# Growth and state products of the first units on VectorE, more filler matmuls, and a new table of positions, in an attention and MLP kernel on one Trainium2 core

## The chip, the core and the metric

The kernel runs on one core of a Trainium2 chip. Its engines are TensorE (PE, with its weight loads as PEld), VectorE (DVE), ScalarE (ACT), GpSimd (POOL) and SyncE (SP); SyncE issues every DMA that matters here. The metric is the device time of one launch in microseconds, median of several runs: 646.78 for the kernel before (three runs, 645.94 to 647.84).

## The reference

A gated linear recurrence with a complex decay runs over 768 steps for 4 batches of 8 heads with head size 48. Its output is the input of an MLP of width 384 to 2048 to 384.

```python
mag = np.sqrt(a_re * a_re + a_im * a_im)
scale = np.minimum(mag, 0.999) / (mag + 1e-06)
...
for t in range(S):
    ...
    S_re, S_im = (new_re + kv, new_im)
    y[:, :, t] = np.einsum('bhd,bhde->bhe', q[:, :, t], S_re)
...
h = x @ w_in
sp = np.where(h > 20.0, h, np.log1p(np.exp(np.minimum(h, 20.0))))
g = h * np.tanh(sp)
return (g @ w_out).astype(np.float32)
```

## The kernel before

The sequence is cut into 12 units of 256 steps (three to a batch), each of two chunks of 128. A unit passes through three blocks of work.

- **Elementwise** (`ew_steps`). From `a_re` and `a_im` it makes the running magnitude (scans at line 333, exponentials on ScalarE, tile X) and the running angle (scans at line 347, reduction to one turn at lines 353 to 358, sine and cosine in `X1` and `R` on ScalarE). `grow` (line 378) multiplies q and k, in tile QK, by the two exponentials in X; this is the growth product. Two tiny copies on GpSimd (lines 380 and 381) follow. `rot` (line 400) then makes four products with sine and cosine, and `relay` (line 391) sends the results by DMA into tile T, with heads and real and imaginary parts on the partitions: per unit six DMAs `T<-X` and six `T<-QK`.
- **Attention** (`attn_steps`). Per chunk: transposes of k (`pkn`, line 465), the products of q and k (`pa`, line 473, masked into `am` on VectorE at line 476), the output in `ypsum` (line 489), and the state update `upd`: matmuls `pd` (line 505), a copy or addition on VectorE (lines 509 and 511), then the product S times the decay at the chunk's end (line 513); this is the S product. `fin` copies the unit's output with four DMAs `xf<-y` (line 524) and splits it into a high part `xH` (ScalarE) and a low part `xL` (VectorE, line 159).
- **MLP** (`moe_steps`). Eight pairs of steps per unit: 18 matmuls into `ph` (line 551), a chain over ScalarE and VectorE (lines 556 to 561, results `g`, `gh`, `gl`), 12 matmuls into `po` (line 581).

The weights arrive as 64-bit floats and are converted in 24 pieces, w_in in `raw`, w_out in `wraw` (two buffers): one ScalarE copy, two VectorE operations (lines 191 and 195), one integer addition on GpSimd (line 200), one cast on ScalarE or VectorE (line 158), one subtraction on VectorE (line 159). Units 0 and 1 run their MLP in halves, since the second halves of the weights come later.

Which engine makes a product is fixed in the code: the growth product is on VectorE for unit 0 alone and on GpSimd for all others, the S product likewise. `spin` issues matmuls on constant data into a scratch bank, whose result nobody reads; they keep TensorE busy. There are 18 before the first attention, after the first angle reduction (`turned[0]`), and 12 more behind unit 0's last attention output (`copied[0]`).

The order of all work comes from a plan: each step is put at a number (the tables EW, AT, LD, WP give first and last positions for a unit's elementwise steps, attention steps, loads and weight conversions), and ES, TS, WS, MB and the per-step table SHIFT move the step's priority. A scheduler then writes one instruction list per engine, SyncE's DMA list among them; each engine works through its list in order and waits at an entry whose inputs are not there.

Of the kernel before, what the change touches and what calls it, by code (L numbers as in the profile page):

```python
# [22 lines left out]
ALU = mybir.AluOpType  # L23
# [18 lines left out]
GACT = 0  # L42
GATE = -1
GRP = 2
RG, QG, GN = 5, 1, 0
SQ0, SORD, CGA, CGN, CGD, ACTG = 1, 0, 9, 3, 0, 0
YDVE = []
RQ = [(), ()]
LG, WG = 12, 12
W1 = 0  # L50
ADDV = 12
NACT, MAGP = 2, 0
ROTU = 2
ROTP = [2]
TREE = 1
WRB, WI = 2, 512
FIN0 = -3.09
FS = 0.0
TRUNC = 0
AFTERX = 0  # L60
# [2 lines left out]
MULP = 0  # L63
LONG = 2
WIDE = 1
WREP, WREP2, WK = 18, 12, -8.6
FAST = [0, 1]
EW = [(-16.09, -10.95), (-12.73, -8.83), (-13.6, -11.78), (-17.88, -11.79), (-16.56, -10.6)]
AT = [(-7.62, -4.55), (-3.79, -0.81), (-8.05, -2.82), (-8.41, -3.06), (-10.49, -2.73)]
WP = [(-7.98, -3.4), (-2.51, 2.77), (1.94, 7.2), (9.3, 9.35)]  # L70
WS = [-3.58, -1.77, 0.05, 1.02]
ES = [3.85, -0.83, -1.67, 1.33]
TS = [0.58, -1.31, 2.46, -0.05]
MB = [-1.21, -0.14]
WL1 = -1.83
SHIFT = {32: -0.19, 113: 0.04, 229: 0.63, 252: 0.1}
RB = 2
XB, X1B = 2, 2
LD = [(-17.86, -17.24, -16.49), (-18.78, -19.85, -19.81), (-17.97, -17.71, -17.6), (-21.23, -15.07, -17.56), (-24.18, -15.85, -17.38)]
WL = 512  # L80
XRUNS = ((0, 0, 0, 32), (0, 1, 32, 16), (64, 1, 64, 16), (0, 2, 80, 32))
LOW, HIGH, FADED = 0.55, 2e6, 1e-17
# [5 lines left out]
def tile_kernel(ctx, tc, q, k, v, are, aim, w_in, w_out, out):  # L88
    nc = tc.nc
# [141 lines left out]
    def ew_steps(u):  # L231
# [141 lines left out]
        def both(x, g):  # L373
            return x[:, g].rearrange("p j a t -> p (j a) t" if isinstance(g, int) else "p c j a t -> p (c j a) t")

        def grow(g):
            QK, X = both(st["QK"], g), both(st["X"], g)
            (nc.vector if g in FAST and u == 0 else nc.gpsimd).tensor_tensor(  # L378
                QK[..., :C], QK[..., :C], X[..., :C], ALU.mult)
            nc.gpsimd.tensor_copy(QK[..., C:], X[..., C - 1:C])  # L380
            nc.gpsimd.tensor_copy(X[..., C:], X[..., C - 1:C])
            q2 = flat(st["QK"][:, :, :, 0], g)[:, :, C]
            cnt = ew.tile([P, NJ * NCH], F32, tag="cnt", name="cnt", bufs=1)
            nc.vector.tensor_scalar(cnt[:, :q2.shape[1]], q2, FADED, 0.0, ALU.is_ge, ALU.add,
                                    accum_out=good[:, gi(g), 2:3])
# [58 lines left out]
    def attn_steps(u):  # L444
# [8 lines left out]
        def chunk(c):  # L453
            first = uu == 0 and c == 0
            last = uu == NU - 1 and c == NCH - 1
            cs = slice(c * C, (c + 1) * C)
            d = {}

            def kn(g):
                def f():  # L460
                    if g == 0:
                        d["kn"] = at.tile([P, H, 2 * D], F32, tag="kn", name="kn")
                    pt = bank([P, 4, 2 * D], "kn", "pkn", c)
                    for i in range(4):
                        nc.tensor.transpose(pt[:, i, :], st["T"][c][:, 4 * g + i, 1, :C], ident[:2 * D, :2 * D])
                    nc.scalar.copy(d["kn"][:, 4 * g:4 * g + 4, :], pt)
                return f

            def amat(g):
                def f():  # L470
                    pa = bank([P, 4, C], "am", "pa", c)
                    for i in range(4):
                        nc.tensor.matmul(pa[:, i, :], st["T"][c][:, 4 * g + i, 1, :C],  # L473
                                         st["T"][c][:, 4 * g + i, 0, :C], start=True, stop=True)
                    am = d["am", g] = at.tile([P, 4, C], F32, tag="am", name="am", bufs=2)
                    nc.vector.tensor_tensor(
                        am, pa, cmask.unsqueeze(1).broadcast_to([P, 4, C]), ALU.mult)
                return f

            def yv(g):  # L480
                def f():
                    py = ypsum
                    for i in (2 * g, 2 * g + 1):
                        for n, old in enumerate(((True, False), (False, True))[u < WIDE] if not first else (False,)):
                            for par in range(2):
                                h = 2 * i + par
                                lhs = d["S"][:, h, :] if old else st["V"][:, c, h * D:(h + 1) * D]
                                rhs = st["T"][c][:, h, 0, :C] if old else d["am", h // 4][:, h % 4, :]
                                nc.tensor.matmul(py[64 * par:64 * par + D, i, :], lhs, rhs,  # L489
                                                 start=n == 0, stop=first or n == 1)  # L490
                    if g == 1:
                        if c == 0:
                            st["y"] = at.tile([112, 4, TU], F32, tag="y", name="y", bufs=1)
                        ins = (nc.vector.tensor_copy if u < 1 and c in YDVE else nc.scalar.copy)(st["y"][:, :, cs], py)
                        if u == 0 and c == 1:
                            copied.append(ins)
                return f

            def upd():
                nS = at.tile([2 * D, H, D], F32, tag="S", name="S", bufs=2)  # L500
                for g in range(2):
                    pd = bank([2 * D, 4, D], "pd", "pd", c)
                    for i in range(4):
                        h = 4 * g + i
                        nc.tensor.matmul(pd[:, i, :], d["kn"][:, h, :], st["V"][:, c, h * D:(h + 1) * D],  # L505
                                         start=True, stop=True)
                    sl = slice(4 * g, 4 * g + 4)
                    if first:
                        nc.vector.tensor_copy(nS[:, sl, :], pd)
                    else:  # L510
                        nc.vector.tensor_tensor(nS[:, sl, :], pd, d["S"][:, sl, :], ALU.add)  # L511
                pe = st["T"][c][:, :, 0, C].unsqueeze(2).broadcast_to([2 * D, H, D])
                (nc.vector if u < WIDE else nc.gpsimd).tensor_tensor(nS, nS, pe, ALU.mult)  # L513
                state["S"] = nS

            def take():
                d["S"] = state.get("S")

            return ([] if last else [kn(0), kn(1)]), [amat(0), amat(1)], [take, yv(0), yv(1)], [] if last else [take, upd]
# [92 lines left out]
    for u in range(NUN):  # L612
        slot = slots.get(u, range(NPAIR * u, NPAIR * (u + 1)))
        t0 = slot[0]
        place(ew_steps(u), t0 + EW[min(u, len(EW) - 1)][0], t0 + EW[min(u, len(EW) - 1)][1], ES[min(u, 3)])
        for n, f in enumerate(units[u]["load"]):
            x = t0 + LD[min(u, len(LD) - 1)][n]
            plan.append((x, len(plan), f, x))
        asteps = attn_steps(u)
        if u == 0:  # L620
            plan.append((FIN0, len(plan), asteps.pop(), FIN0 + FS))
        place(asteps, t0 + AT[min(u, len(AT) - 1)][0], t0 + AT[min(u, len(AT) - 1)][1], TS[min(u, 3)])
        moe = moe_steps(units[u], u * TU, u, u < 2)
        for j in range(NPAIR):
            plan.append((slot[j], len(plan), moe[0][j], slot[j] + MB[0]))
            plan.append((slot[j] + LAG + 0.5, len(plan), moe[1][j], slot[j] + LAG + 0.5 + MB[1]))
    edge = len(plan)
    plan.append((-15.9, len(plan), load_win(0)))
    plan.append((WL1, len(plan), load_win(1)))
    plan.append((WK, len(plan), spin(WREP, turned)))  # L630
    if WREP2:
        plan.append((FIN0 + 0.01, len(plan), spin(WREP2, copied)))
    n = HALF // WI
    for i, f in enumerate((win, wout)):
        for half in range(2):
            place([f(n * half + m) for m in range(n)], *WP[2 * half + i], WS[2 * half + i])
    def due(x):
        key = x[1] if x[1] < edge else 1000 + x[1] - edge
        return (x[3] if len(x) > 3 else x[0]) + SHIFT.get(key, 0.0), x[1]

# [23 lines left out]
def general(tc, nc, q, k, v, are, aim, pools, moe_steps, split):  # L664
    io, ew, at, ps, dram = (pools[n] for n in ("io", "ew", "at", "ps", "dram"))
    BJ = B * NJ
    TS = 8
    xs = dram.tile([B, S, DM], F32, name="xs")
# [14 lines left out]
    kv, t1, t2, t3, t4 = w1[:, 0], w1[:, 1], w2[:, 0], w2[:, 1], w3  # L683
    n = B * TS * D
    m = BJ * TS
    big = at.tile([P, n + 5 * m], F32, tag="T", name="big", bufs=TB)
    more = at.tile([P, 3 * m + BJ * D], F32, tag="T", name="more", bufs=TB)
    vb = big[:, 0:n].rearrange("p (b t e) -> p b t e", b=B, t=TS)
    cols = [x[:, o + i * m:o + (i + 1) * m].rearrange("p (b j t) -> p b j t", b=B, j=NJ)
            for x, o, cnt in ((big, n, 5), (more, 0, 3)) for i in range(cnt)]  # L690
    cq, ck, cr, ci, cm, ca, cb, cc = cols
    qs = more[:, 3 * m:].rearrange("p (a e) -> p a e", e=D)
    ysb = at.tile([H, B, TS, D], F32, tag="T", name="ysb", bufs=TB)
    tt, ts = nc.vector.tensor_tensor, nc.vector.tensor_scalar
# [132 lines left out]
```

## Time and profile before

| | |
|---|---|
| median of 3 runs | 646.78 us |
| profiled execution, its own time | 646.22 us |
| its span, first to last instruction | 644.4 us |
| mean granted TensorE clock | 0.958 of full speed |
| busy: PE / DVE / ACT / POOL | 579.0 / 500.3 / 493.4 / 124.2 us |

Busy time is the sum over an engine's instructions; the rest of the span it is idle. The page's slices show that TensorE is busy nine tenths or more from about a third of the span on, at the full clock, and less, at changing clocks, before. A granted clock of 1.0 is 2.4 GHz, one of 0.5 is 1.2 GHz. In the rows below a bracket behind an instruction names the idle time before it and what ended that wait.

### The profile page before, as it was taken

To read this page: it belongs to the slowest core of one execution; us is meant where nothing else is said; L and a number is where in the kernel's file an instruction comes from. 1 tells how busy PE (TensorE), PEld (TensorE's weight loads), DVE (VectorE), ACT (ScalarE), POOL (GpSimd) and SP (SyncE) were. 2 spreads that over 40 slices of the span, in tenths; PEclk is the share of its full clock that TensorE was granted. 3 is DMA by queue.
4 is the path that set the end of the run, shared out by engine and by line. 5 is a ranking of instruction groups with operands and counts; after the bars stand their busy time and mean duration, and the time that the engine had idled before them with its cause. 6 is when DMAs were issued, how large, how long until landed. Compare 5 with 4: busy or idle time off the path is not lost.

```text
span 644.4 us, 11738 instructions
## 1 busy us (share of the span) xinstructions
PE 579.0 (90%) x4480; PEld 547.3 (85%) x4480; DVE 500.3 (78%) x859; ACT 493.4 (77%) x789; POOL 124.2 (19%) x99
## 2 busy tenths in 40 slices
PE   0597963987799999999999999999999999999996
PEld 0386853987789999989999999999999999999995
DVE  6979999999879868777878698688588786534451
ACT  7968876877696987978888887888789868655561
POOL 2433364325103103103003112111031030000000
PEclk9958977897899999999999999999999999999999
DMA  8877434514821530630711712703702503101000
GB/s 304 264 255 219 120 115 121 166 37 130 222 64 50 148 100 25 158 89 26 194 54 48 181 45 61 190 22 95 177 23 63 138 14 95 42 25 26 1 26 30
DMA packets 58528, 67.05 MB, mean 104 GB/s; under 512 B 4960, under 2 KB 51040, under 8 KB 58464
## 3 DMA queue, kind: packets, MB, share of 16 engines
q1 hardware_dynamic: 58464, 66.23, 36.1%
q8 instruction: 37, 0.61, 0.4%
q14 instruction: 27, 0.22, 0.1%
HBM read 36.96 MB, written 5.51 MB: 66 GB/s over the span
## 4 chain that ended last, share of the span: by engine, by line
PE 36%; DVE 27%; ACT 17%; DMA 9%; issue 6%; SPq 4%; POOL 1%; DVEq 0%; ACTq 0%; POOLq 0%
PE po L581 14%; PE ph L551 13%; ACT e L124 7%; DVE gl L159 3%; ACT L132 3%; PE ypsum L489 3%; DVE e L556 3%; PE pa L473 3%; DMA T<-QK 3%; SPq L391 3%; ACT X L124 2%; DMA R<-a_re 2%; PE pd L505 2%; DVE g L561 2%; DMA xf<-y 2%
## 5 line engine op out<-in xcount | busy, mean ns | idle before, releaser
L581 PE MATMUL po<-wo,gh 128*128 128x384 f32 x768 | 219.2, 347 | 13.8 <-DVE wo L158 10.4
L551 PE MATMUL ph<-xH,wiH 128*128 128x256 f32 x576 | 168.7, 294 | 3.7 <-DVE g L561 3.6
L551 PE MATMUL ph<-xL,wiH 128*128 128x256 f32 x576 | 165.1, 287 | 4.4 <-DVE xL L159 4.4
L551 PE MATMUL ph<-xH,wiL 128*128 128x256 f32 x576 | 165.5, 288 | 0.0
L581 PEld LDWEIGHTS po<-wo,gh 128*128 128x128 f32 x768 | 141.4, 190 | 18.4 <-DVE wo L158 10.7
L124 ACT ACTIVATE e<-e 128x512 f32<-128x512 f32 x192 | 119.6, 629 | 46.8 <-DVE e L556 44.7
L581 PE MATMUL po<-wo,gl 128*128 128x384 f32 x384 | 131.0, 341 | 0.0
L551 PEld LDWEIGHTS ph<-xH,wiH 128*128 128x128 f32 x576 | 111.5, 194 | 8.4 <-issue 4.8
L551 PEld LDWEIGHTS ph<-xL,wiH 128*128 128x128 f32 x576 | 111.5, 194 | 5.3 <-DVE xL L159 5.2
L551 PEld LDWEIGHTS ph<-xH,wiL 128*128 128x128 f32 x576 | 111.3, 193 | 0.2 <-issue 0.2
L556 DVE TENSOR_SCALAR e<-e 128x512 f32<-128x512 f32 x96 | 55.3, 577 | 40.8 <-ACT e L124 40.5
L561 DVE SCALAR_TENSOR_TENSOR g<-e,ph 128x512 f32<-128x512 f32 x96 | 65.5, 682 | 21.0 <-ACT e L124 20.1
L124 ACT ACTIVATE e<-ph 128x512 f32<-128x512 f32 x96 | 56.6, 590 | 30.8 <-PE ph L551 28.8
L159 DVE TENSOR_TENSOR gl<-g,gh 128x512 fp32r<-128x512 f32 x96 | 74.5, 776 | 1.6
L513 POOL TENSOR_TENSOR S<-S,T 96x384 f32<-96x384 f32 x18 | 26.6, 1476 | 240.0 <-DVE S L511 91.6
L581 PEld LDWEIGHTS po<-wo,gl 128*128 128x128 f32 x384 | 72.8, 190 | 0.0
L124 ACT ACTIVATE e<-e,fifth 128x512 f32<-128x512 f32 x96 | 69.1, 720 | 1.8
L158 DVE CAST gh<-g 128x512 fp32r<-128x512 f32 x96 | 42.8, 445 | 33.9 <-PE po L581 32.6
L378 POOL TENSOR_TENSOR QK<-QK,X 128x1536 f32<-128x1536 f32 (+1 forms) x12 | 40.9, 3412 | 123.8 <-ACT X L124 123.8
L132 ACT ACT_TABLE_LOAD x45 | 57.7, 1283 | 1.6 <-PEq L783 0.8
L473 PE MATMUL pa<-T 96*128 96x128 f32 x384 | 51.4, 283 | 4.5 <-DVE S L511 3.4
L473 PEld LDWEIGHTS pa<-T 96*128 96x128 f32 x384 | 48.3, 197 | 5.2 <-DVE S L511 3.5
(88 smaller groups left out, 820.1 us busy)
## 6 DMA issues: line engine op xcount, KB each, us to landing
T<-X SPq DMA_DIRECT2D x72, 129.0 KB, 2.5
T<-QK SPq DMA_DIRECT2D x72, 129.0 KB, 4.3
raw<-w_in SPq DMA_DIRECT2D x12, 512.0 KB, 8.2
wraw<-w_out SPq DMA_DIRECT2D x12, 512.0 KB, 3.6
QK<-q SPq DMA_DIRECT2D x12, 384.0 KB, 4.0
QK<-k SPq DMA_DIRECT2D x12, 384.0 KB, 4.7
V<-v SPq DMA_DIRECT2D x12, 384.0 KB, 4.9
out_dram<-o SPq DMA_DIRECT2D x24, 192.0 KB, 1.9
```

The lines of the kernel that those rows point to most:

```text
L124: ins = nc.scalar.activation(out, in_, func, **kw)
L132: ins = nc.scalar.preload_act_table_set(name)
L158: heng(h, src)
L159: leng(out=lo, in0=src, in1=h.bitcast(F32), op=ALU.subtract)
L378: (nc.vector if g in FAST and u == 0 else nc.gpsimd).tensor_tensor(QK[..., :C], QK[..., :C], X[..., :C], ALU.mult)
L391: ins = (nc.gpsimd if u == 0 and 3 * cs + j in RQ[c] else nc.sync).dma_start(rows[cs * NJ + j], src[:, c, j])
L473: nc.tensor.matmul(pa[:, i, :], st["T"][c][:, 4 * g + i, 1, :C], st["T"][c][:, 4 * g + i, 0, :C], start=True, stop=True)
L513: (nc.vector if u < WIDE else nc.gpsimd).tensor_tensor(nS, nS, pe, ALU.mult)
L551: nc.tensor.matmul(ph[:, a, :], wi[wp][:, j, kt, a * P:a * P + P], st[xp][:, kt, :], start=n == 0, stop=n == 8)
L556: nc.vector.tensor_scalar_min(e, e, math.exp(20.0))
L561: nc.vector.scalar_tensor_tensor(g, e, 2.5, ph, ALU.subtract, ALU.mult)
L581: nc.tensor.matmul(po[t], gp[:, a, tsl], wo[part][:, wp, 2 * i + a, :], start=j in starts and a == 0 and n == 0, stop=j + 1 in ends and a ...
```

## The change

Growth products of units 1 to 3 and S products of units 1 and 2 go from GpSimd to VectorE. The rounding of the angle in units 0 and 1 (line 353, ScalarE) becomes line 355 on VectorE (NACT). The fillers grow from 18 to 24 and from 12 to 18. Conversion of the first weights is ordered behind unit 0's first four rotation products (CGD), unit 1's first squares behind unit 0's sines (ACTG), and the second half of w_in is no longer held behind unit 1's q and k loads and unit 0's output copy (QG, RG). All positions are new, and SHIFT has 74 entries where it had 4.

```diff
-RG, QG, GN = 5, 1, 0
-SQ0, SORD, CGA, CGN, CGD, ACTG = 1, 0, 9, 3, 0, 0
+RG, QG, GN = 9, 0, 0
+SQ0, SORD, CGA, CGN, CGD, ACTG = 1, 0, 9, 3, 4, 1
-NACT, MAGP = 2, 0
+NACT, MAGP = 0, 0
-FIN0 = -3.09
+FIN0 = -2.9
-WREP, WREP2, WK = 18, 12, -8.6
-FAST = [0, 1]
-EW = [(-16.09, -10.95), (-12.73, -8.83), (-13.6, -11.78), (-17.88, -11.79), (-16.56, -10.6)]
-AT = [(-7.62, -4.55), (-3.79, -0.81), (-8.05, -2.82), (-8.41, -3.06), (-10.49, -2.73)]
...
+WREP, WREP2, WK = 24, 18, -9.4
+FASTU, FASTE, SPE = 4, 99, 3
+EW = [(-15.98, -11.16), (-12.71, -8.85), (-13.64, -11.75), (-17.88, -11.94), (-16.2, -10.54)]
+AT = [(-9.7, -6.15), (-4.54, -2.43), (-8.86, -3.46), (-7.13, -3.62), (-10.18, -2.73)]
...
-SHIFT = {32: -0.19, 113: 0.04, 229: 0.63, 252: 0.1}
...
-LD = [(-17.86, -17.24, -16.49), (-18.78, -19.85, -19.81), (-17.97, -17.71, -17.6), (-21.23, -15.07, -17.56), (-24.18, -15.85, -17.38)]
+LD = [(-16.55, -15.97, -14.96), (-17.84, -19.05, -19.66), (-18.09, -17.59, -17.24), (-20.15, -13.15, -18.75), (-24.2, -15.53, -17.4)]
...
-            (nc.vector if g in FAST and u == 0 else nc.gpsimd).tensor_tensor(
+            (nc.vector if u < FASTU or u >= FASTE else nc.gpsimd).tensor_tensor(
                 QK[..., :C], QK[..., :C], X[..., :C], ALU.mult)
...
-                (nc.vector if u < WIDE else nc.gpsimd).tensor_tensor(nS, nS, pe, ALU.mult)
+                (nc.vector if u < SPE else nc.gpsimd).tensor_tensor(nS, nS, pe, ALU.mult)
```

The table of numbers tells a reader nothing of the order, so three places of the instruction lists follow, before and with the change. The first is VectorE's list around unit 2's growth product, from the unit's magnitude scan on (R: magnitude and then cosine, X: exponentials, wiL and wo: weights). Before:

```order
L333 SCALAR_TENSOR_TENSOR R<-rmask,R 128x768
L355 TENSOR_SCALAR I<-X_738 128x768
L195 SCALAR_TENSOR_TENSOR wraw<-wraw,wx 128x512
L561 SCALAR_TENSOR_TENSOR g<-e,ph 128x512
L159 TENSOR_TENSOR xL<-xf,xH 128x256 x3
L356 SCALAR_TENSOR_TENSOR I<-X_738,I 128x768
L191 TENSOR_SCALAR wx<-raw_99 128x512
L158 CAST gh<-g 128x512
L195 SCALAR_TENSOR_TENSOR raw_99<-raw_99,wx 128x512
L159 TENSOR_TENSOR gl<-g,gh 128x512
L159 TENSOR_TENSOR wo_491<-wraw,wo_491 128x512
L191 TENSOR_SCALAR wx<-wraw 128x512
```
With the change:

```order
L333 SCALAR_TENSOR_TENSOR R<-rmask,R 128x768
L355 TENSOR_SCALAR I<-X_794 128x768
L561 SCALAR_TENSOR_TENSOR g<-e,ph 128x512
L159 TENSOR_TENSOR xL<-xf,xH 128x256 x2
L195 SCALAR_TENSOR_TENSOR wraw<-wraw,wx 128x512
L159 TENSOR_TENSOR wiL<-raw_99,wiH 128x512
L159 TENSOR_TENSOR xL<-xf,xH 128x256
L356 SCALAR_TENSOR_TENSOR I<-X_794,I 128x768
L158 CAST gh<-g 128x512
L378 TENSOR_TENSOR QK<-QK,X 128x12x128
L384 TENSOR_SCALAR cnt,good<-QK 128x6
L191 TENSOR_SCALAR wx<-raw_99 128x512
```
The product L378, which GpSimd made before and which is not in VectorE's list before, now stands nine rows behind the scan L333 whose exponentials it needs, in front of the check of its result (L384).

The second place is SyncE's list where unit 3's relays, unit 2's output copies `xf<-y` and the next loads meet. Before:

```order
L391 DMA T<-X 16x8x258 x2
L219 DMA wraw<-w_out 128x512
L391 DMA T<-X 16x8x258 x4
L391 DMA T<-QK 16x8x258 x6
L263 DMA V<-v 128x768
L248 DMA R<-a_re 128x768
L256 DMA QK<-q 128x6x128
L524 DMA xf<-y 128x1x256
L524 DMA xf<-y 64x1x256 x2
L524 DMA xf<-y 128x1x256
L256 DMA QK<-k 128x6x128
```
With the change:

```order
L391 DMA T<-X 16x8x258
L219 DMA wraw<-w_out 128x512
L391 DMA T<-X 16x8x258 x5
L391 DMA T<-QK 16x8x258 x2
L263 DMA V<-v 128x768
L391 DMA T<-QK 16x8x258 x3
L524 DMA xf<-y 128x1x256
L524 DMA xf<-y 64x1x256 x2
L524 DMA xf<-y 128x1x256
L391 DMA T<-QK 16x8x258
L248 DMA R<-a_re 128x768
L256 DMA QK<-q 128x6x128
```
The output copies stood behind the loads V, R and q; now they stand in front of R and q and of the last relay.

The third is the same list one unit later (relays of unit 4, loads of R two units ahead), and it repeats for five more units with the load of R at a similar place. Before:

```order
L248 DMA I<-a_im 128x768
L391 DMA T<-X 16x8x258 x6
L524 DMA xf<-y 128x1x256
L524 DMA xf<-y 64x1x256 x2
L524 DMA xf<-y 128x1x256
L263 DMA V<-v 128x768
L391 DMA T<-QK 16x8x258 x6
L248 DMA R<-a_re 128x768
```
With the change:

```order
L248 DMA I<-a_im 128x768
L391 DMA T<-X 16x8x258 x4
L248 DMA R<-a_re 128x768
L391 DMA T<-X 16x8x258 x2
L524 DMA xf<-y 128x1x256
L524 DMA xf<-y 64x1x256 x2
L524 DMA xf<-y 128x1x256
L263 DMA V<-v 128x768
L391 DMA T<-QK 16x8x258 x6
```
The load of R moved from behind the twelve relays to behind the fourth of them.

## Rows read from the trace of the kernel before

**Rows 1.** Five stretches: us, busy (count) of PE, PEld, DVE, ACT, POOL, clock, DMA share, GB/s.

```profile
20.00:50.00 30.00, 25.26 (x151) 18.24 (x150) 26.25 (x53) 24.48 (x51) 13.01 (x9) 0.73 0.74 242
50.00:110.00 60.00, 42.20 (x313) 36.49 (x311) 58.79 (x90) 46.14 (x74) 29.10 (x19) 0.87 0.50 143
110.00:160.00 50.00, 41.63 (x285) 39.54 (x286) 50.00 (x81) 38.13 (x60) 18.66 (x12) 0.84 0.36 107
160.00:182.00 22.00, 17.27 (x127) 16.06 (x126) 17.03 (x30) 15.08 (x29) 2.57 (x2) 0.92 0.75 193
182.00:600.00 418.00, 413.64 (x3353) 399.15 (x3352) 316.80 (x546) 333.77 (x519) 56.70 (x39) 1.00 0.31 82
```

**Rows 2.** Chain that ended last, 0 to 52 us: start us, us, what.

```profile
4.93 6.64 DMA raw<-w_in
18.67 0.51 ACT I L353
```

**Rows 3.** The same chain, 80 to 185 us.

```profile
159.84 5.47 DMA wraw<-w_out
173.50 4.17 DMA xf<-y
```

**Rows 4.** GpSimd (POOL) in order of time: start us, us, instruction [idle before].

```profile
93.19 3.66 POOL L378 TENSOR_TENSOR QK<-QK,X 128x1536 f32<-128x1536 f32 x1
144.46 4.15 POOL L378 TENSOR_TENSOR QK<-QK,X 128x1536 f32<-128x1536 f32 x1 [6.42 <-ACT X L124]
154.19 1.03 POOL L513 TENSOR_TENSOR S<-S,T 96x384 f32<-96x384 f32 x1
```

**Rows 5.** VectorE (DVE) in order of time, beside those GpSimd instructions.

```profile
93.43 3.69 DVE L159 TENSOR_TENSOR xL<-xf,xH 128x256 fp32r<-128x256 f32 x1
145.16 3.46 DVE L358 COPY ncar<-I 128x3 f32<-128x3 f32 x1
154.44 1.07 DVE L158 CAST gh<-g 128x512 fp32r<-128x512 f32 x1
```

**Rows 6.** VectorE instructions grouped by line and form: count, busy us, mean ns, idle before.

```profile
L378 DVE TENSOR_TENSOR QK<-QK,X 128x768 f32<-128x768 f32 x2 | 1.9, 960 | 0.8 <-ACT X L124 0.8
L328 DVE TENSOR_SCALAR X<-X 128x384 f32<-128x384 f32 x2 | 0.8, 418 | 0.0
L513 DVE TENSOR_TENSOR S<-S,T 96x384 f32<-96x384 f32 x2 | 1.1, 568 | 0.0
L159 DVE TENSOR_TENSOR xL<-xf,xH 128x256 fp32r<-128x256 f32 x27 | 11.1, 420 | 3.5 <-ACT xH L158 3.3
L358 DVE COPY ncar<-I 128x3 f32<-128x3 f32 x5 | 0.8, 160 | 0.0
L158 DVE CAST gh<-g 128x512 fp32r<-128x512 f32 x96 | 42.8, 445 | 33.9 <-PE po L581 32.6
```

**Rows 7.** VectorE in order of time, 30 to 50 us, with its idle time.

```profile
38.68 0.35 DVE L509 COPY S<-pd 96x192 f32<-96x192 f32 x1 [1.60 <-PE pd L505]
43.84 0.35 DVE L511 TENSOR_TENSOR S<-pd,S 96x192 f32<-96x192 f32 x1 [0.93 <-PE pd L505]
```

**Rows 8.** DMA issues of SyncE (SPq) in order of time.

```profile
4.08 0.81 SPq L263 DMA_DIRECT2D V<-v  x1
172.16 2.57 SPq L524 DMA_DIRECT2D xf<-y  x4
```

**Rows 9.** ScalarE and TensorE in order of time, near 169 us.

```profile
168.62 0.56 ACT L494 COPY y<-ypsum 112x512 f32<-112x512 f32 x1
169.54 0.85 PE L465 MATMUL pkn<-ident,T 96*128 96x96 f32 x8 [3.55 <-DMA T<-QK]
```

**Rows 10.** Waits of TensorE, 170 to 600 us: total us, times, longest us.

```profile
PE pkn L465 <- DMA T<-QK: 4.4, 6, 1.0
```

**Rows 11.** DMA issues of SyncE in a later unit, 260 to 275 us.

```profile
261.90 3.20 SPq L391 DMA_DIRECT2D T<-X  x5
273.63 0.59 SPq L248 DMA_DIRECT2D R<-a_re  x1
```

More of the change, by code (lines that the diff above doesn't have):

```diff
@@ L65 @@
 WIDE = 1
-WREP, WREP2, WK = 18, 12, -8.6
-FAST = [0, 1]
-EW = [(-16.09, -10.95), (-12.73, -8.83), (-13.6, -11.78), (-17.88, -11.79), (-16.56, -10.6)]
-AT = [(-7.62, -4.55), (-3.79, -0.81), (-8.05, -2.82), (-8.41, -3.06), (-10.49, -2.73)]
[L70 to L75, printed above, removed]
-SHIFT = {32: -0.19, 113: 0.04, 229: 0.63, 252: 0.1}
+WREP, WREP2, WK = 24, 18, -9.4
+FASTU, FASTE, SPE = 4, 99, 3
+EW = [(-15.98, -11.16), (-12.71, -8.85), (-13.64, -11.75), (-17.88, -11.94), (-16.2, -10.54)]
+AT = [(-9.7, -6.15), (-4.54, -2.43), (-8.86, -3.46), (-7.13, -3.62), (-10.18, -2.73)]
+WP = [(-7.65, -3.07), (-2.97, 3.2), (1.47, 6.47), (8.4, 9.09)]
+WS = [-4.02, -0.78, -1.58, 0.97]
+ES = [5.11, 0.98, -3.54, 3.14]
+TS = [3.1, -0.68, 2.63, 0.06]
+MB = [-1.26, -0.4]
+WL1 = -1.85
+SHIFT = {1: 2.1, 7: 0.15, 8: -0.08, 9: 0.94, 11: -0.03, 14: 0.15, 19: -0.4, 28: 1.75, 32: -0.15, 35: 1.52, 42: -0.93, 48: 2.06, 55: -0.02, 65: -1.84, 70: 0.48, 71: 0.82, 78: -2.74, 79: 0.12, 88: -0.29, 91: -1.5, 97: -1.09, 98: -0.09, 100: -0.72, 105: 0.19, 109: 0.06, 112: -0.15, 113: 0.04, 115: -0.04, 121: 0.46, 122: -1.01, 155: -0.24, 175: 3.45, 218: 0.53, 225: 0.58, 229: 0.63, 240: -0.02, 248: 0.12, 252: 0.1, 257: -0.08, 263: 0.15, 277: 0.42, 305: -0.27, 308: -1.62, 320: 0.06, 334: -1.12, 341: -0.38, 348: -0.25, 358: -1.22, 359: -1.81, 366: 0.03, 374: -0.4, 382: -0.71, 384: -1.52, 387: 0.68, 389: 0.47, 398: 1.17, 417: 0.98, 437: 0.86, 439: -1.18, 443: -0.35, 455: 0.49, 471: 0.2, 1001: -0.1, 1002: -0.54, 1007: -0.17, 1008: 1.15, 1010: 2.05, 1014: -0.35, 1015: -0.05, 1018: -1.41, 1019: -0.45, 1021: 0.09, 1026: -2.4, 1027: -3.57}
 RB = 2
 XB, X1B = 2, 2
-LD = [(-17.86, -17.24, -16.49), (-18.78, -19.85, -19.81), (-17.97, -17.71, -17.6), (-21.23, -15.07, -17.56), (-24.18, -15.85, -17.38)]
+LD = [(-16.55, -15.97, -14.96), (-17.84, -19.05, -19.66), (-18.09, -17.59, -17.24), (-20.15, -13.15, -18.75), (-24.2, -15.53, -17.4)]
 WL = 512
```

## The prediction

> **What bounds the kernel now.** I read the busy time by stretches first [rows 1]. From 182 to 600 us TensorE is busy 413.64 of 418 at the full clock; VectorE and ScalarE have a fifth of their time free. There only TensorE's own waits can be won. Before that it is otherwise: from 50 to 160 us VectorE is busy 58.79 of 60 and 50.00 of 50, while TensorE has 26 us free and a lower clock. VectorE's list is the bound of that stretch, and the chain that ended last runs along it until 159.84 us, where it passes to a DMA of w_out and, by the relays, to unit 2's output copies at 173.50 [rows 3]. Ahead of 50 us the chain goes through the first load of w_in and the angle roundings on ScalarE [rows 2]. So the time is: a head of some 50 us, 110 us of VectorE, 22 us of hand-over, then TensorE.
>
> The sum is made against the profiled execution's own 646.22 us (span 644.4); the median of the runs is 0.56 above it, which I add at the end. A measurement of this kernel tells a change from none from about 0.3% on, 1.9 us: faster is below 644.8, slower above 648.7.
>
> **VectorE from 50 to 160 us.** What comes on: no row shows the growth product of a whole unit, 128x1536, on VectorE; half of it takes 960 ns [rows 6]. Twice that, 1.92, for unit 2 and the same for unit 3, and three S products (two of unit 1, one of unit 2) at 568 ns [rows 6], 1.70: together 5.54 us, all on the bound.
>
> What goes away: while GpSimd makes these products, VectorE stands. Its subtraction xL takes 3.69 beside unit 2's growth product, and the copy of three columns 3.46 beside unit 3's [rows 4, 5]; elsewhere they take 0.42 and 0.16 [rows 6]. That is 3.27 and 3.30 back. Beside unit 2's S product a cast takes 1.07 [rows 5] against 0.445 [rows 6], 0.63 back; I count two such (the third S product falls beside operations that hardly stretch), 1.25. Together 7.8. Net: **-2.3 us**. Bounds: only the two long stalls come back, 6.57 against 5.54, -1.0; or the whole length of GpSimd's products, 3.66 and 4.15 and three of 1.03 [rows 4], 10.9, net -5.4. I take the value from the rows where VectorE's stretching was seen.
>
> The list order agrees with this: unit 2's product stands nine rows behind the scan, and between them lie seven operations of 0.4 to 1 us, longer than ScalarE's two exponentials need, so VectorE should not stand at the product. The next late thing, if the stalls go, is the angle of unit 2 on VectorE, which stood behind the stalled xL and gains by the same amount.
>
> Unit 1's growth product, twice 0.96, falls near 40 to 45 us, where VectorE waits 1.60 and 0.93 for TensorE [rows 7]. That covers it: nothing. Without that cover it costs 1.9.
>
> **The head.** In units 0 and 1 the angle rounding leaves ScalarE (0.51 each, on the chain [rows 2]) for VectorE, 0.42 by the nearest row, a 128x384 operation with one scalar pair [rows 6]; it also saves two hand-overs, but the second group's next step now stands behind two rotation products. I count half a microsecond for the first group alone. The load of V, 0.81 of SyncE's time, stood ahead of w_in [rows 8] and goes behind it; the first w_in piece ends the chain's DMA [rows 2], so it can come 0.8 earlier. Together **-1.3**, between -2.0 and 0 (VectorE may be busy with other conversions).
>
> **The fillers.** Six more in front of the first attention lie before a wait for relays, six more behind unit 0's output before waits for xL; I count nothing. If they held the clock at full from 20 to 50 us, where it is 0.73 on average with TensorE busy 25.26 [rows 1], up to 6.8 could come; if they delay unit 0's MLP by their own length, some 1.5 could go. The row nearest to the fillers is TensorE's idle wait behind them, so zero.
>
> **160 to 182 us.** Unit 2's output is copied to y by 169.18 [rows 9], but its DMAs go out only at 172.16 [rows 8], behind loads that wait for buffers. In SyncE's new list they stand ahead of those loads, so up to 3.0 us sooner. TensorE has other matmuls for most of this, and one wait of 3.55 for the relays [rows 9]. I take half, **-1.5**, between 0 and -3.6.
>
> **182 to 600 us.** TensorE waits six times for `T<-QK` relays, 4.4 us in all [rows 10]; nothing else there is worth counting. Behind each such unit lies a chain that starts with a load of R. In the new list R is issued behind the fourth of the `T<-X` relays instead of behind all twelve: in the unit at 262 us that is some 9 us sooner (273.63 against about 264.5 [rows 11]). I take two thirds of the waits as won, **-3.0**, between 0 and -4.4.
>
> Sum: -1.3 - 2.3 - 1.5 - 3.0 = -8.1, so 638.1 on the profiled execution and **638.7 us** on the median.
>
> **The skill, where it speaks against this.** The stalls in [rows 5] say that an idle-looking GpSimd costs a full VectorE more than the product itself. The Trainium skill, Perfetto Trace Analysis, section Optimizing Scalar/DVE Operations, says that with VectorE saturated it may make sense to offload work to GpSimd, though it adds that this might not help, since the two share a port. By its first half the 5.54 would simply be paid; that is the even case below.
>
> **Rivals.**
> - *The whole length comes back.* If an operation of VectorE that meets a GpSimd product loses all of it, 10.9 goes instead of 7.8: 3.1 better, 635.6; with the far ends of the other terms (-2.0, -3.6, -4.4 and -5.4 in the sum), 631.4. For it: two stalls were nearly as long as the products. Against: unit 1's products at 41 to 46 us stalled little. By the Trainium skill, SBUF — State Buffer, section Who interferes with whom, the loser of the shared pair of ports blocks fully for the whole instruction. Chance 0.16.
> - *Even.* The work is paid and the stalls return elsewhere, because GpSimd keeps its 24 integer additions and meets other operations of VectorE with them: 646.8 - 5.8 + 5.5 = 646.5. Against: the stall of a short addition is a fraction of that of a growth product. Chance 0.15.
> - *R in front of the relays, slower.* Place: SyncE's list in units 4 to 9. The load of R two units ahead reuses the buffer that this unit's rotation products still read, and SyncE waits at its entry. Two relays of X and all of QK are behind it. Price: 0.6 for the issue alone [rows 11] up to 2.2 with its 384 KB at the 242 GB/s of [rows 1], say 1.4 in each of six units, 8.4, every microsecond of which TensorE feels, since it already waits for these relays [rows 10]. 646.8 - 5.1 + 8.4 = 650.1. It decides where the rotation's two QK products (0.96 each [rows 6]) end later than four relays of X take to issue (3.20 for five, so 2.6 [rows 11]). Two products are 1.9, so by the rows the wait is just avoided, unless something stands between them in VectorE's list. Chance 0.21.
> - *That the change does not do what it says* is excluded for the moved products by the lists; for the fillers it is the zero that I took.
>
> **The numbers.** My forecast has 0.48, with its own range 634 to 644.8. With the whole-length case faster has 0.64, the even case 0.15, slower 0.21. The range takes in most of the first two cases, the even one, and the slower one with some more than its price: 630 to 652. Below it I leave 0.08, above it 0.08.
>
> **What would show it.** Right: in the new profile xL and the column copy take 0.4 and 0.2 everywhere before 180 us; the growth product on VectorE shows 1.9 per unit; VectorE is still busy nine tenths or more from 50 to 155; its last wo subtraction comes some 3 to 4 us earlier; the four `xf<-y` of unit 2 go out right behind the copy to y; TensorE's waits for `T<-QK` shrink to 1 to 2 us. Wrong: new long stalls beside the integer additions (even case); SyncE's entry for R waiting longer than half a microsecond in units 4 to 9, with TensorE's waits at 8 us or more (slower case); a gain that lies ahead of 50 us at a full clock (the fillers, which I priced at nothing).

## The result and the profile after

The change takes 637.73 us in the median of 4 runs (636.66 to 641.35), the kernel before 646.51 on the same chip (645.94 to 647.84): ratio 0.9865, 95% interval 0.9827 to 0.9902, so 8.8 us faster. The forecast was 638.7 us, between 630 and 652. The profiled execution took 636.66 us, with a span of 634.8, 9.6 less than before.

The stretches of [rows 1] in the changed kernel, in the same columns:

```profile
20.00:50.00 30.00, 23.75 (x156) 16.18 (x155) 29.70 (x63) 25.59 (x52) 8.04 (x8) 0.85 0.81 262
50.00:110.00 60.00, 43.51 (x327) 37.07 (x325) 58.94 (x97) 47.70 (x75) 20.42 (x15) 0.90 0.52 148
110.00:160.00 50.00, 45.97 (x329) 43.26 (x328) 49.82 (x84) 36.25 (x57) 16.76 (x12) 0.91 0.41 117
160.00:182.00 22.00, 19.04 (x139) 18.73 (x139) 16.76 (x32) 19.23 (x35) 1.04 (x1) 0.92 0.61 159
182.00:600.00 418.00, 414.60 (x3358) 401.10 (x3358) 313.44 (x544) 331.43 (x519) 56.92 (x39) 1.00 0.29 81
```

VectorE is as full as before from 50 to 160 us, but gets through more instructions there: 181 against 171. TensorE is busy 7.4 us more in the three stretches from 50 to 182 us, and 1.0 more from 182 to 600.

The moved products and the two operations that stood beside them before, VectorE grouped by form over the whole execution (count, busy us, mean ns, idle before):

```profile
L378 DVE TENSOR_TENSOR QK<-QK,X 128x768 f32<-128x768 f32 x4 | 3.8, 951 | 0.1
L378 DVE TENSOR_TENSOR QK<-QK,X 128x1536 f32<-128x1536 f32 x2 | 3.5, 1745 | 0.0
L513 DVE TENSOR_TENSOR S<-S,T 96x384 f32<-96x384 f32 x5 | 2.7, 542 | 0.0
```

and xL and the column copy from 50 to 182 us:

```profile
L159 DVE TENSOR_TENSOR xL<-xf,xH 128x256 fp32r<-128x256 f32 x9 | 3.6, 416 | 0.0
L358 DVE COPY ncar<-I 128x3 f32<-128x3 f32 x1 | 0.2, 208 | 0.0
```

A whole unit's product takes 1.745 us, and the 3.69 and 3.46 of [rows 5] are 0.42 and 0.21.

Where the time came from is read from the same pieces of work in both traces. Unit 0's second copy to y starts at 46.9 us in both, to 0.1. The first matmul of the 13th gate block (18 matmuls each, 96 in all) is 1.3 us earlier, at 143.4; that of the 14th 4.5 earlier, at 149.1; that of the 17th, which is unit 2's first, 8.7 earlier, at 172.7; the end is 9.6 earlier. What comes between the 13th and the 14th is a wait of TensorE for VectorE's state addition (S, line 511). Before, then with the change:

```profile
151.08 2.08 PE L473 MATMUL pa<-T 96*128 96x128 f32 x8 [3.35 <-DVE S L511]
```

```profile
147.88 1.16 PE L473 MATMUL pa<-T 96*128 96x128 f32 x8 [1.07 <-DVE S L511]
```

So **some 4.4 us appear by the end of the stretch that VectorE bounds, 4.2 at the hand-over and 0.9 behind it**. At the hand-over TensorE's list stands in another order. Before, the transposes of unit 3's keys (pkn) stand ahead of the 15th gate block and wait 3.55 [rows 9]. Now the block goes first, and the transposes behind it do not wait:

```profile
162.96 0.39 PE L551 MATMUL ph<-xH,wiH 128*128 128x256 f32 x1 [3.43 <-DVE g L561]
166.35 1.22 PE L465 MATMUL pkn<-ident,T 96*128 96x96 f32 x8
```

SyncE's issues there in the changed kernel (not all of them); [rows 8] had the output copies at 172.16:

```profile
148.57 0.33 SPq L219 DMA_DIRECT2D wraw<-w_out  x1
153.51 0.53 SPq L219 DMA_DIRECT2D wraw<-w_out  x1
154.09 3.28 SPq L391 DMA_DIRECT2D T<-X  x5
157.47 1.22 SPq L391 DMA_DIRECT2D T<-QK  x2
163.63 2.54 SPq L524 DMA_DIRECT2D xf<-y  x4
```

TensorE's waits from 170 to 600 us, the view of [rows 10]:

```profile
PE po L581 <- ACT o L596: 1.9, 1, 1.9
PE pkn L465 <- DMA T<-QK: 1.4, 2, 1.2
```

### The profile page after: what moved, and what is told of

Same layout as the page of the kernel before. It is cut to its first block, busy times and chain, and to the rows that moved or that the text cites. A ratio compares the mean times of both kernels' runs of the same rounds, so it can differ in the third digit from the quotient of the medians.

```text
span 634.8 us, 11779 instructions
## 1 busy us (share of the span) xinstructions
PE 576.3 (91%) x4492; PEld 544.6 (86%) x4492; DVE 494.2 (78%) x870; ACT 489.5 (77%) x785; POOL 107.2 (17%) x92
## 4 chain that ended last, share of the span: by engine, by line
PE 52%; DVE 24%; ACT 10%; DMA 6%; issue 4%; SPq 3%; DVEq 0%; ACTq 0%
PE po L581 20%; PE ph L551 20%; PE ypsum L489 4%; ACT e L124 4%; PE pa L473 3%; PE pd L505 2%; DVE gl L159 2%; DMA raw<-w_in 2%; ACT L132 2%; DVE e L556 2%; DVE X L347 2%; DMA T<-X 2%; DVE g L561 2%; ACT X L124 2%; DVE gh L158 1%
## 5 line engine op out<-in xcount | busy, mean ns | idle before, releaser
L581 PE MATMUL po<-wo,gh 128*128 128x384 f32 x768 | 215.6, 344 | 3.4 <-ACT o L596 1.9
L556 DVE TENSOR_SCALAR e<-e 128x512 f32<-128x512 f32 x96 | 52.1, 545 | 24.3 <-ACT e L124 24.0
L513 POOL TENSOR_TENSOR S<-S,T 96x384 f32<-96x384 f32 x15 | 23.6, 1574 | 212.9 <-DVE S L511 139.5
L378 POOL TENSOR_TENSOR QK<-QK,X 128x1536 f32<-128x1536 f32 x8 | 28.5, 3565 | 129.1 <-ACT X L124 129.1
```

The lines of the kernel that those rows point to most:

```text
L378: (nc.vector if u < FASTU or u >= FASTE else nc.gpsimd).tensor_tensor(QK[..., :C], QK[..., :C], X[..., :C], ALU.mult)
L513: (nc.vector if u < SPE else nc.gpsimd).tensor_tensor(nS, nS, pe, ALU.mult)
L556: nc.vector.tensor_scalar_min(e, e, math.exp(20.0))
L581: nc.tensor.matmul(po[t], gp[:, a, tsl], wo[part][:, wp, 2 * i + a, :], start=j in starts and a == 0 and n == 0, stop=j + 1 in ends and a ...
```

## The experiments

The theory: the growth products on GpSimd stall VectorE, whose list is the bound up to 160 us, and from there the lateness goes on to the hand-over. The rivals: the new positions made the gain, and the engine of the products is even; the fillers made it, by the clock; or the earlier load of R did. Twelve kernels tell these apart. In the table a ratio is to the kernel before, run beside it on the same chip (the runs were on several chips); the last column is its distance to the change's 0.9865, times 646.5 us. The change's own interval is 2.5 us wide to either side, the others' 1.2 to 2.3, so distances below some 3 us are not secured by the times alone.

| kernel | median us | ratio (95%) | against the change, us |
|---|---|---|---|
| growth of units 1 to 3 back on GpSimd | 647.97 | 0.9992 (0.9961 to 1.0023) | +8.2 |
| growth of units 2 and 3 back | 645.00 | 0.9964 (0.9946 to 0.9982) | +6.4 |
| growth of unit 3 back | 643.46 | 0.9951 (0.9926 to 0.9977) | +5.6 |
| the same, gate block first | 641.82 | 0.9909 (0.9878 to 0.9939) | +2.8 |
| S products back | 640.02 | 0.9879 (0.9846 to 0.9911) | +0.9 |
| all products back, new positions alone | 645.76 | 0.9972 (0.9942 to 1.0002) | +6.9 |
| products alone, positions of before | 644.07 | 0.9945 (0.9915 to 0.9975) | +5.2 |
| fewer fillers | 638.59 | 0.9878 (0.9849 to 0.9908) | +0.8 |
| R late | 639.19 | 0.9869 (0.9842 to 0.9895) | +0.3 |
| transposes first | 640.56 | 0.9902 (0.9871 to 0.9933) | +2.4 |
| late step on w_out | 640.48 | 0.9895 (0.9863 to 0.9928) | +1.9 |
| growth of all units on VectorE | 633.07 | 0.9789 (0.9753 to 0.9824) | -4.9 |

**Growth products of units 1 to 3 back on GpSimd.**

```diff
-FASTU, FASTE, SPE = 4, 99, 3
+FASTU, FASTE, SPE = 1, 99, 3
```

> The change, with the growth products of units 1 to 3 back on GpSimd. Theory A (the products on GpSimd stall VectorE by their own length, and VectorE's list is the bound to 160 us): unit 2's and unit 3's products give VectorE 2 x 1.74 us back but cost stalls of 3.3 us or more each, seen as single operations of 3 to 4 us beside them; unit 1's are covered. Time 637.7 + 6.6 - 3.5 = 640.8, at least 639.0; the last w_out subtraction is 2 to 3 us later than in the change. Rival B (the new positions made the gain, and the engine of the products is even): 637.7 within 1.0, stalls there or not. Rival C (GpSimd would have been the better place, and the positions paid for the products): 635 or less.

It lost 8.2 us, nearly all of the 8.8 that the change had won (A had about 3). The stalls are back, one operation beside each product. GpSimd in order of time, and VectorE:

```profile
92.46 3.72 POOL L378 TENSOR_TENSOR QK<-QK,X 128x1536 f32<-128x1536 f32 x1 [7.91 <-ACT X L124]
142.24 3.70 POOL L378 TENSOR_TENSOR QK<-QK,X 128x1536 f32<-128x1536 f32 x1 [11.86 <-ACT X L124]
```

```profile
93.35 3.65 DVE L356 SCALAR_TENSOR_TENSOR I<-X,I 128x768 f32<-128x768 f32 x1
143.14 3.35 DVE L159 TENSOR_TENSOR gl<-g,gh 128x512 fp32r<-128x512 f32 x1
```

They hit other operations than before (L356 takes 0.95 alone, gl 0.69), at 2.7 us each. Rival B, that the products are even, falls. But A's sum falls too: two stalls of 2.7 less two products of 1.74 are 1.9 us of VectorE, and 8.2 came of it.

**S products back.**

```diff
-FASTU, FASTE, SPE = 4, 99, 3
+FASTU, FASTE, SPE = 4, 99, 1
```

> The change, with the S products of units 1 and 2 back on GpSimd (three of them). Theory A: three products of 0.57 us leave VectorE, 1.7 us, and two or three stalls of 0.6 us come, 1.25 to 1.9: 637.7 within 0.8. Rival B (positions): the same, 637.7. Rival C (each product costs its whole length on GpSimd, 1.03 us, as a stall, and the state is later for the attention too): 639 to 640.

0.9 us, no difference that can be told. A and B both had nearly this, and C's 1.3 to 2.3 lie within the uncertainty too. Of the moved products, then, only the growth products have a price that the times show.

**All products back.**

```diff
-FASTU, FASTE, SPE = 4, 99, 3
+FASTU, FASTE, SPE = 1, 99, 1
```

> The change without any moved product: new positions, fillers and load order alone. Theory A: the product move is worth 2 to 3 us of the 8.8, so 640 to 641, and 646.5 - 640.5 = 6 us are due to positions, loads and fillers. Rival B (positions alone): 637.7 within 1.0. Rival D (the positions were only worth something together with the products, because they were found for them): 643 or more.

The new positions, loads and fillers alone give 0.0028, or 1.8 us, and the interval still holds none. A's 6 us for them was wrong; D is the one that fits.

**Products alone, at the positions of before.**

```diff
-            (nc.vector if g in FAST and u == 0 else nc.gpsimd).tensor_tensor(
+            (nc.vector if u < 4 else nc.gpsimd).tensor_tensor(
...
-                (nc.vector if u < WIDE else nc.gpsimd).tensor_tensor(nS, nS, pe, ALU.mult)
+                (nc.vector if u < 3 else nc.gpsimd).tensor_tensor(nS, nS, pe, ALU.mult)
```

> The kernel before, with the growth products of units 0 to 3 and the S products of units 0 to 2 on VectorE, and nothing else changed. Theory A: 646.5 - 2.3 = 644.2 (between 641 and 645.5), xL of unit 2 and the column copy of unit 3 at 0.4 and 0.2 us in place of 3.69 and 3.46. Rival B (the engine of the products is even): 646.5 within 1.0, the stalls gone and as much VectorE work in their place. Rival D (the moved products at the old positions come at bad places, VectorE waits for ScalarE at them): 648 or more.

3.6 us faster than before: A's direction and its span of 641 to 645.5, and both named stalls are gone (xL 0.41, the column copy 0.15). Alone the parts give 3.6 and 1.8, together 8.7. The 3.3 that they give only together are not secured by the intervals, but the traces show one thing that only the two together bring: in the kernel before, with the products alone and with the positions alone, the transposes stand ahead of the 15th gate block; in the change they stand behind it.

**One unit after the other.** The same table entry, at 3 and at 2:

```diff
-FASTU, FASTE, SPE = 4, 99, 3
+FASTU, FASTE, SPE = 3, 99, 3
```

> The change, with the growth product of unit 3 alone back on GpSimd. All three back cost 8 to 10 us. Theory A (a product on GpSimd costs its own extra length on the way to unit 3's relays, and stalls VectorE too; at the hand-over TensorE waits for unit 3's relays directly): most of it here, 4 to 6 us slower than the change, with TensorE's wait at 163 to 168 us longer by 3. Rival B (the stalls alone: each of units 2 and 3 costs what VectorE loses less 1.74): 1.5 to 2 us. Rival C (it is not the product but the list that the scheduler makes when it sits on GpSimd): less than 1.

```diff
-FASTU, FASTE, SPE = 4, 99, 3
+FASTU, FASTE, SPE = 2, 99, 3
```

> The change, with the growth products of units 2 and 3 back on GpSimd and unit 1's on VectorE. Theory A: unit 3's 4 to 6 and unit 2's stall less 1.74, about 1.5: 6 to 8 us slower than the change; what is left to all three, about 2, is unit 1's. Rival B (stalls alone): 3 to 4. Rival D (unit 1's product, which I had held covered, makes most of the loss): 2 or less.

Unit 3's product costs 5.6 of the 8.2, which is A's span; unit 2's adds 0.8 and unit 1's 1.8, each within the uncertainty, so D, that unit 1's makes most of it, falls. In the trace of the second of these kernels VectorE is not stalled beside unit 2's product. There GpSimd is the one that stands, 7.67 us in place of some 3.5, and VectorE then waits for the result. GpSimd, then VectorE:

```profile
92.97 7.67 POOL L378 TENSOR_TENSOR QK<-QK,X 128x1536 f32<-128x1536 f32 x1 [4.24 <-ACT X L124]
```

```profile
100.82 0.16 DVE L384 TENSOR_SCALAR_CACHE_REDUCE cnt<-QK 128x6 f32<-128x6 f32 x1 [3.55 <-POOL QK L380]
```

In the trace of unit 3's return VectorE loses little: GpSimd's product takes 3.49, and so does the column copy beside it; the change has 1.745 and 0.21 there, so 1.5 us less. Yet TensorE stands 8.62 where it stood 3.43. GpSimd, VectorE and TensorE of that kernel:

```profile
139.57 3.49 POOL L378 TENSOR_TENSOR QK<-QK,X 128x1536 f32<-128x1536 f32 x1 [8.49 <-ACT X L124]
```

```profile
139.60 3.49 DVE L358 COPY ncar<-I 128x3 f32<-128x3 f32 x1
```

```profile
167.78 1.51 PE L465 MATMUL pkn<-ident,T 96*128 96x96 f32 x8 [8.62 <-DMA T<-QK]
```

With the product on another engine all lists are planned anew from there on, and the transposes stand first again, waiting for unit 3's relays with 18 matmuls behind them. So the next two runs took this place in TensorE's list by itself.

**Transposes first, products on VectorE.** Only the order of TensorE's list there is fixed; SyncE's and GpSimd's lists stay as they are in the change, ScalarE's and VectorE's do so until 178 us.

```diff
+                            if unit == 1 and j == 6:
+                                block.append(ins)
...
+                        if u == 3 and c == 0:
+                            after(block[0], ins)
```

> The change, its products on VectorE, with one thing turned round in TensorE's list at the hand-over: the eight transposes of unit 3's keys, which wait for the relays of QK, stand ahead of the 18 matmuls of the next gate block instead of behind them, as they do in the kernel before and with unit 3's product on GpSimd. Theory A (the place in the list is a part of the 5.6 us that unit 3's product cost when put back): the wait at 163 us grows from 3.4 to about 6 us, and the kernel is 2 to 3 us slower than the change, some 6 us under the kernel before. Rival B (the list's order is worth nothing, TensorE finds the same work later): within 1.0 of the change. Rival C (the order is all of it): 5 us or more slower.

```profile
165.07 1.30 PE L466 MATMUL pkn<-ident,T 96*128 96x96 f32 x8 [4.75 <-issue]
```

2.4 us slower, with a wait of 4.75 for 3.43 and unit 2's first block at 174.8 for 172.7. That is A's amount, but the interval reaches to B's.

**Unit 3 back, gate block first.** The other way round, with `FASTU` at 3:

```diff
+                        if u == 3 and c == 0:
+                            after(ins, block[-1])
```

> Unit 3's growth product on GpSimd, as in the run that cost 5.6 us, with TensorE's list at the hand-over held as in the change: the 18 matmuls of the gate block ahead of the transposes. Theory A: 2 to 3 of the 5.6 come back; what is left, about 3, is the stall of the column copy and the later relays. Rival B (list worth nothing): 5.6 slower than the change as before. Rival C (the list is all): within 1.0 of the change.

2.7 of the 5.6 us came back, again A's amount. The two runs agree on some 2.5 us of unit 3's price for the place in the list, though neither distance is secured by the times alone: unit 2's first gate block comes 3.0 us sooner than in unit 3's plain return (176.1 against 179.2), but the two profiled executions end together (spans 639.9 and 640.0). One run speaks against a fixed price: with the S products back the transposes also stand first, and that kernel is only 0.9 us slower. What is left, 2.8, can be followed in part. VectorE in order of time, then SyncE, ScalarE and TensorE of this kernel (the edit shifts its line numbers a little):

```profile
140.02 3.45 DVE L359 COPY ncar<-I 128x3 f32<-128x3 f32 x1
```

```profile
153.69 0.33 SPq L220 DMA_DIRECT2D wraw<-w_out  x1
155.24 0.53 SPq L220 DMA_DIRECT2D wraw<-w_out  x1
155.82 3.25 SPq L392 DMA_DIRECT2D T<-X  x5
```

```profile
161.39 0.69 ACT L124 ACTIVATE wraw<-wraw 128x512 int32<-128x512 uint32 x1 [1.43 <-DMA wraw<-w_out]
```

```profile
166.68 0.58 PE L554 MATMUL ph<-xH,wiH 128*128 128x256 f32 x1 [4.73 <-DVE g L566]
```

The last load of w_out goes out 1.7 us later than the 153.51 of the change, the relays behind it 1.7 later too; ScalarE's step on that load, at 159.18 in the change, is 2.2 later, the gate block behind it 3.7. So a microsecond and a half on VectorE has become 3.7 on TensorE. That it grows because each next step stands in a list behind another late one is argued and not tried, and it has a rival: only TensorE's order was held here. VectorE's, SyncE's and ScalarE's lists differ from the change's too, and the load of w_out before the last, at 148.57 in the change, goes out at 153.69, 5.1 later, now behind other entries of SyncE's list. How much of the 2.8 is lateness and how much these lists stays open.

**Fewer fillers.**

```diff
-WREP, WREP2, WK = 24, 18, -9.4
+WREP, WREP2, WK = 18, 12, -9.4
```

> The change, with 18 and 12 filler matmuls as before in place of 24 and 18. Theory A (they lie in TensorE's idle waits): 8.7 us under the kernel before, within 1.0, and unit 0's first gate matmul within 0.5 us. Rival C (they keep the granted clock up, 0.85 from 20 to 50 us in the change against 0.73 before): the clock of that stretch falls and 2 to 4 us are lost. Rival D (they delay unit 0's MLP, whose first matmul came 1.3 us later in the change): that matmul comes 1.3 us sooner, and the time falls by up to 1.3.

Windows from 20 to 50 us of this kernel:

```profile
20.00:50.00 30.00, 22.91 (x156) 16.47 (x154) 29.66 (x62) 26.14 (x54) 9.11 (x9) 0.89 0.83 267
```

0.8 us, no difference that can be told. The clock was 0.89 with fewer fillers, against 0.85, so C falls. D is half right: unit 0's first gate matmul came at 49.8 instead of 53.0 (1.9 of that from an earlier copy to y in this execution), but unit 0's first output matmul only 0.8 us earlier, and the end not at all.

**R late.**

```diff
+                    if u >= 6 and n == "R":
+                        after(ins, units[u - 2]["relays"][-1])
...
+                    st.setdefault("relays", []).append(ins)
```

> The change, with the load of R of units 6 to 11 held in SyncE's list behind the last relay of QK of the unit two before, as it stood before the change. Theory A (the early R shortens the chain that ends in TensorE's waits for relays): those waits rise from 1.4 us in the stretch from 182 us to 3 us or more, and the time rises by 1 to 3 us; not by more, since the end came only 1.0 us further ahead there in the whole change. Rival B (transfers of R are hidden anyway): within 1.0 us of the change, 8.7 under the kernel before.

SyncE's issues of one unit, first of the change, then of this kernel:

```profile
253.35 1.90 SPq L391 DMA_DIRECT2D T<-X  x3
255.36 0.53 SPq L248 DMA_DIRECT2D R<-a_re  x1
256.00 1.87 SPq L391 DMA_DIRECT2D T<-X  x3
```

```profile
256.06 3.85 SPq L393 DMA_DIRECT2D T<-X  x6
265.10 2.56 SPq L393 DMA_DIRECT2D T<-QK  x4
267.71 0.59 SPq L248 DMA_DIRECT2D R<-a_re  x1
```

and its waits of TensorE from 182 us on:

```profile
PE po L584 <- ACT o L599: 2.7, 3, 1.3
PE pkn L468 <- DMA T<-QK: 0.5, 1, 0.5
```

R goes out 11.7 us behind the first relays instead of 2.0, the time is the same within 0.3, and the waits for `T<-QK` are 0.5, less than the change's 1.4. A's sign, waits of 3 us or more, did not come; B is the one that fits: the transfer is hidden.

**Late step on w_out.** An attempt at the 3.43 us that TensorE still waits: ScalarE stands 2.71 for a w_out load there, with the exponentials of the waiting gate block behind it.

```diff
+                if unit == 0 and j == 7:
+                    after(converted[-1], ins)
```

> The change, with ScalarE's step on the last w_out block put behind the exponentials of the gate block that waits, so that ScalarE does not stand 2.7 us for that load with TensorE idle behind it at 159.5 to 163.0 us. If that wait is what holds TensorE there, its idle time falls from 3.4 to about 1 us and the kernel is 1 to 2.5 us faster than the change. Rival: the relays of QK behind it end at the same time, TensorE waits for them instead, within 0.7 of the change.

Not faster; 1.9 slower, within the uncertainty. The block came 1.1 us earlier, at 161.9, and TensorE then waited 1.44 at 165.7 and 0.99 at 172.9; the edit also changed SyncE's list in a later unit, and the waits for `T<-QK` rose from 1.4 to 2.9. Whether the step alone would help stays open.

**Growth of all units on VectorE.**

```diff
-FASTU, FASTE, SPE = 4, 99, 3
+FASTU, FASTE, SPE = 4, 4, 3
```

> The change, with the growth products of all twelve units on VectorE. Theory A (the engine of the product matters only where VectorE's list is the bound; from 182 us on TensorE is): within 1.5 us of the change, TensorE's waits from 182 us on about as before. Rival D (VectorE's stalls beside GpSimd reach TensorE there too, 1.9 us at 383 us behind a subtraction of 4.67): 2 to 3 us faster. Rival E (24 to 28 more us of product time in VectorE's list... eight of 1.74, about 14 in all, come into the way of the gate blocks): 2 us or more slower.

4.9 us faster than the change, 13.6 (0.0211) faster than before; its interval, up to 0.9824, lies just below the change's, and the profiled spans are 3.5 us apart. To 182 us its trace is that of the change (unit 2's first gate block at 172.7 in both). Then comes the gain. Windows and grouped products of this kernel:

```profile
182.00:600.00 418.00, 417.16 (x3376) 404.06 (x3376) 310.98 (x554) 333.54 (x523) 38.37 (x31) 1.00 0.29 81
```

```profile
L378 DVE TENSOR_TENSOR QK<-QK,X 128x1536 f32<-128x1536 f32 x10 | 17.5, 1750 | 0.0
```

Eight more products, 14 us, went to VectorE, and it is busy 2.5 us less from 182 to 600 us. TensorE's idle time there falls from 3.4 to 0.84. The stalls account for it: over VectorE's instructions that start there, the time above the median of the same form in the same kernel is 18.8 us in the change and 2.4 here, 16.4 less for 14 more of products. A, that the engine matters only where VectorE is the bound, falls; D is right, with its 2 to 3 us in TensorE's idle time and somewhat more in the median. From 195 us on its lists are in part planned anew, which is not separated from this. The costliest place in the change shows how. GpSimd, VectorE and TensorE of the change:

```profile
377.00 3.49 POOL L378 TENSOR_TENSOR QK<-QK,X 128x1536 f32<-128x1536 f32 x1
```

```profile
376.36 4.67 DVE L159 TENSOR_TENSOR gl<-g,gh 128x512 fp32r<-128x512 f32 x1
```

```profile
383.06 0.44 PE L581 MATMUL po<-wo,gh 128*128 128x384 f32 x1 [1.88 <-ACT o L596]
```

The subtraction meets an S product and the growth product one after the other, and ScalarE, and TensorE's output matmuls behind it, wait. With the products on VectorE this wait is gone.

## Why the prediction was right, and where it was not

The time was right to 1 us, the terms were not: two were too small, two too large, and that they made up for each other is luck. By place, read from the same pieces of work in both traces (unit 0's copy to y, the 14th and the 17th gate block, the end):

| place | forecast, us | profiled executions, us |
|---|---|---|
| the head | -1.3 | -0.1 |
| VectorE's stretch | -2.3 | -4.4 |
| hand-over | -1.5 | -4.2 |
| from there on | -3.0 | -0.9 |

**What bounds the kernel** held: VectorE is full from 50 to 160 us after the change too, and what it loses there is paid by TensorE.

**VectorE, -2.3.** The mechanism was right: products on GpSimd stall VectorE by nearly their length, and both named stalls went. VectorE's last subtraction on w_out starts 4.7 us earlier (167.9 against 172.6), where 3 to 4 was named for a sign. The mis-sized step is "together 5.54 us, all on the bound" against "together 7.8". The time that VectorE's instructions from 50 to 160 us take above the median of the same form in the same kernel, worked out from the traces, is 22.2 us before, 12.9 with the change, 13.5 with the products alone and 19.1 with the positions alone. So 9.3 us of stall went with the change, more than 7.8, for about 5.1 us of products (two of 1.745, three of 0.542). With the products alone 8.7 went, 3.6 net, and that kernel is 3.6 us faster: there the sum holds as it was meant, one microsecond of VectorE's list for one of time.

In the new positions it does not. There the growth products are worth 8.2 us by their return, 5.6 of it unit 3's, for 1.5 to 1.9 us of VectorE; some 2.5 us go with the order that the scheduler gave TensorE, and the rest with late steps and other new lists, not separated. The size of a product was also a little high, 1.92 for 1.745, and between the scan and the product stand nine operations, not seven. That the whole length comes back is a rival that fits the stalls, but its 3 us would not have made 8.2 either. The S products, half a microsecond in that sum, cannot be told from zero.

The even case is excluded by the first run. The Trainium skill, Perfetto Trace Analysis, section Optimizing Scalar/DVE Operations, allows an offload to GpSimd when VectorE is saturated, with the doubt that the shared port may undo it; here the doubt was right, 8.2 us of it. The Trainium skill, SBUF — State Buffer, section Who interferes with whom, has the loser of the shared ports block for the other's whole instruction, and the trace agrees, 3.49 beside 3.49; in one trace GpSimd was the loser (the 7.67 above).

**Unit 1's product, nothing**: 1.8 by the table, between the 0 and the 1.9 that it names, not settled.

**The head, -1.3**: nothing came. The step that failed is "so it can come 0.8 earlier". The chain's first load in the change:

```profile
4.80 7.86 DMA raw<-w_in
```

took 7.86 where it took 6.64 [rows 2], and landed 1.1 us later although SyncE issued w_in 0.8 earlier. The DMA engines are full there in both kernels (a share of 0.95 and 0.98 from 4 to 8 us), and an earlier issue bought no earlier landing; which transfer took its place I did not follow. The rounding left ScalarE as said, and unit 0's y came at the same time.

**The fillers, 0**: right as far as the run with fewer can tell.

**160 to 182 us, -1.5**: here 4.2 us came, and the reason that I gave is at most a small part of them. The four `xf<-y` do go out right behind the copy to y, as named, but the 8.2 us of the growth products, the 2.5 of the list's order among them, leave little of the 8.8 for them. What their place alone is worth was not tried.

**182 to 600 us, -3.0**: the steps that failed are "Behind each such unit lies a chain that starts with a load of R" and "two thirds of the waits as won". R did go out that much sooner, and the waits for `T<-QK` shrank by the 3.0 of the forecast, to 1.4, as I had named for a sign. But with R put back they stay small, so the sign did not test the cause, and TensorE's busy time rose by only 1.0, since a new wait of 1.9 behind the stalled subtraction at 376 us took most of it. The slower rival, R in front of the relays, did not come either: in all six units R goes out right behind the fourth relay, with no wait.

So -8.1 stands against -9.6 between the profiled executions and -8.8 between the medians: VectorE's stretch 2.1 us under and the hand-over 2.7; from there on 2.1 over, the head 1.2 over. With the growth products back the 14th gate block comes 1.5 us later than in the change, at 150.6, and the 15th 6.1 later, at 169.1: their return takes about a third of what VectorE's stretch had won and all of the hand-over's. The 1.5 for the hand-over's loads is borne out by no run by itself.

## What to carry to other kernels

Where an operation can sit on VectorE or GpSimd, put the stall that it causes into the sum, also where VectorE has a fourth of its time free: eight products of 1.75 us made VectorE's busy time shorter, not longer. An operation that changes its engine changes the lists of the others too, and at the hand-over from one stage to the next that weighed here as much as the stall or more: compare the lists, and follow them to the engine that waits. And a sign that would follow from several causes proves none of them: undo the one part and look again.

## What was not expected of the hardware

A growth product on GpSimd took 3.5 us (up to 4.15 before, once 7.67 where GpSimd was the one that stood) and one on VectorE 1.75, a factor of 2.0; the surprise was that moving eight of them made VectorE's busy time from 182 to 600 us fall by 2.5 (313.44 to 310.98). The granted clock from 20 to 50 us was 0.85 and 0.77 in two kernels with the same fillers, 0.89 with fewer and 0.70 with R late, and none of it shows in the times. Single executions of the kernel before lay between 642.7 and 652.2 us, 1.5% apart, so a distance of 2 us needed the order of the work in the trace beside the time.
